# Gated attention and spatial-shift MLP mixer: a fixed engine order in the first token mixing block, fillers, and the MLP's first normalisation between the w2 products

## The chip, the cores and the metric

The kernel runs on one NeuronCore of a Trainium2 chip. The metric is the device time of one execution in microseconds (us). A core has five engines that matter here: TensorE (PE, matrix products; its weight loads are listed as PEld), VectorE (DVE), ScalarE (ACT, which evaluates functions such as gelu and exp from tables), GpSimd (POOL) and SyncE (SP, which here only issues DMA transfers). Each engine works through its own queue in order. Where it needs what another engine makes, it waits for a semaphore, and everything behind it in its queue waits too.

## The reference

```python
g  = sigmoid((x * gate_w).sum(-1))                # per token
# A: attention, 16 heads of 28 columns, one shared K and V
q = (x @ wq) -> 16 heads;  k = x @ wk;  v = x @ wv
a = softmax(q k^T * 28**-0.5) v -> concat -> @ wo
# B: spatial-shift mixer and MLP
h  = gelu(layernorm(x) @ w1)
hs = concat(h0 shifted +1, h1 shifted -1, h2 shifted +2, h3 shifted -2 tokens) @ w2
x1 = x + hs
b  = x1 + gelu(layernorm(x1) @ w3) @ w4
out = g * a + (1 - g) * b
```

x has S = 2048 tokens of D = 448 columns in fp32; w3 and w4 have an inner width of 1792. The layernorm has no scale or offset.

## The kernel before

Tokens are worked in 4 blocks of 512, each block in 4 tiles of 128 (16 tiles in all). To keep fp32 accuracy, most operands are split into a high part and a low remainder (names ending in h and l), and a product is summed from three: high by high, high by low, low by high. `proj` (L113 to L119) is one such sum of 11 matmuls over the 448 contracted columns. The fourth slice of 64 columns carries low parts in its other half, which saves one.

The work has three stages.

Stage 1, token mixing (about 0 to 130 us of the span). `stage_kv` (L247) makes k, v and the gate's sum in one product per block; `stage_q` (L278) makes the first two groups of q, whose parts are copied out by `q_evac` (L144: qh on ACT, ql on DVE, three DMAs to qs); `stage_v` (L270) transposes v into vext and the gate's sum into gz. The layernorm of block b is `ln1_begin` (L284), whose `layernorm_stats` (L121) runs four bn_stats and bn_aggr on DVE (L126, L127) and an add and a power on POOL (L128, L129) to get rs; and four `layernorm_tile` (L132): the normalised tile xn on DVE (L135), a copy of its last 64 columns on POOL (L137), four transposes on PE into tile tp (L140), and `split_a` (L108 to L111), which makes ah on ACT and al on DVE. `stage_w1` (L293) multiplies by w1 in four parts m, runs the normalisation tiles of the next block between them, and applies gelu twice on ACT (L304, L305); the low part hl comes from POOL (L306). `stage_w2` (L317) makes four tiles of the shifted product, 12 matmuls each (L322 to L324), and DVE adds each to x (L326). Lines 330 to 354 give the order. At its end the first MLP block is prepared: `ln_begin(0)`, `load_w34(i)` for the first four of seven pairs of w3 and w4 columns, and `ln_tile(0, t)` (the MLP's use of `layernorm_tile`). `load_w34` (L360) issues a DMA for w3 and one for w4 into a single buffer each, and splits them (w3h and w4h on ACT at L101 and L370, w3l on DVE at L104 and L105, w4l on POOL at L371). The order there is w2 of block 2, v of block 3, the further loads, `ln_tile(0, 0)`, then w2 of block 3 with the other three `ln_tile` between its tiles.

Stage 2, the MLP (about 130 to 424 us). For each block, 14 parts f: the product g with w3 (the lines of `proj`, L115 to L119), gelu twice (L409, L410), the low part gl (L411), and 12 matmuls with w4 into four accumulators (L419 to L421). At the end of a block DVE adds the accumulators to x (L449). Products of score maxima for the attention fill gaps.

Stage 3, attention (424 us to the end). First come the gate and the weights: gg = exp(-gz) on ACT (L456), gg + 1, its reciprocal, gi = 1 - gg on DVE (L457 to L459); wq is split (L576 to L587, high parts on DVE, low parts on POOL), the first block of x is loaded and split (`load_x(0)`, L483 to L491: ahq on DVE, alq on POOL), wo is split on POOL (L592, L593), and each tile of x is multiplied by gi on POOL (L595, L596: 16 instructions). The main loop (L646) runs 16 units of 16 key tiles: scores s on PE (L663), exp on ACT (L665), products with V on PE (L625). Further jobs are fed between the scores, a product at a time, by `pump`; the first is the q product of unit 2 (`q_job`, L493 to L509), from key tile 7 of the first unit on. Its second matmul (L503) reads alq.

PE's order is the order in which the code is written (a manual schedule of PE). The order of the other engines is chosen when the program is built, by a list scheduler that works by estimated times; an instruction written late may be put early if its inputs are there. So L456 and the first scalings of L596, which are written in stage 3, run during stage 2.

Of the kernel before, what the change touches and what calls it, by code (L numbers as in the profile page):

```python
# [15 lines left out]
P = 128  # L16
S = 2048
D = 448
# [17 lines left out]
def f32(ap):  # L36
    return ap.bitcast(F32)
# [3 lines left out]
def gated_mix_kernel(  # L41
# [32 lines left out]
    powt = keep.tile([P, 4], F32, name="powt")  # L74
    sel8 = keep.tile([P, P], F32R, name="sel8")
    mcs = [keep.tile([P, P], F32R, name=f"mc_{i}") for i in range(2)]
    nc.gpsimd.memset(epst, EPS)
    nc.gpsimd.memset(powt, -0.5)
    nc.gpsimd.memset(vext, 0.0)
    nc.gpsimd.memset(vext[:, :, 0:1], 1.0)  # L80
    nc.gpsimd.memset(f32(kS)[96:128, :], 1.0)
# [10 lines left out]
    def misc_tile(name):  # L92
        return psA.tile([P, 512], F32, tag="misc", bufs=1, name=name)

    wps = misc_tile("warm_ps")
    for _ in range(30):
        nc.tensor.matmul(wps[:, 0:256], warm[:, 0:P], warm, start=True, stop=True)

    def split_w(raw, wh, wl, eng=None):
        eng = eng or nc.vector  # L100
        nc.scalar.copy(wh[:, 0:3, :], raw[:, 0:3, :])  # L101
        nc.scalar.copy(wh[0:64, 3, :], raw[0:64, 3, :])
        nc.gpsimd.memset(f32(wh)[64:128, 3, :], 0.0)
        eng.tensor_tensor(wl[:, 0:3, :], raw[:, 0:3, :], f32(wh)[:, 0:3, :], ALU.subtract)  # L104
        eng.tensor_tensor(wl[0:64, 3, :], raw[0:64, 3, :], f32(wh)[0:64, 3, :], ALU.subtract)  # L105
        nc.scalar.copy(wl[64:128, 3, :], raw[64:128, 3, :])
# [6 lines left out]
    def proj(ps, wh, wl, ah, al):  # L113
        for c in range(3):
            nc.tensor.matmul(ps, wh[:, c, :], ah[:, c, :], start=(c == 0), stop=False)  # L115
            nc.tensor.matmul(ps, wh[:, c, :], al[:, c, :], start=False, stop=False)  # L116
            nc.tensor.matmul(ps, wl[:, c, :], ah[:, c, :], start=False, stop=False)  # L117
        nc.tensor.matmul(ps, wh[:, 3, :], ah[:, 3, :], start=False, stop=False)  # L118
        nc.tensor.matmul(ps, wl[:, 3, :], ah[:, 3, :], start=False, stop=True)  # L119
# [9 lines left out]
        nc.gpsimd.tensor_tensor(rs, rs, powt, ALU.pow)  # L129
        return mv, rs  # L130

    def layernorm_tile(pool, tp_of, b, t, mv, rs, ah, al):  # L132
        xt = x1[:, 4 * b + t, :]
        xn = pool.tile([P, 512], F32, tag="xn", bufs=3, name=f"xn_{pool.name}_{b}_{t}")
        nc.vector.tensor_scalar(xn[:, 0:D], xt, mv[:, t, 0:1], rs[:, t:t + 1],  # L135
                                op0=ALU.subtract, op1=ALU.mult)
        nc.gpsimd.tensor_copy(xn[:, D:512], xn[:, 384:D])  # L137
        tp = tp_of(f"tp_{pool.name}_{b}_{t}").rearrange("p (c n) -> p c n", c=4)
        for c in range(4):
            nc.tensor.transpose(tp[:, c, :], xn[:, c * P:(c + 1) * P], ident)  # L140
        cols = slice(t * P, (t + 1) * P)
        split_a(tp, ah[:, :, cols], al[:, :, cols])

    def q_evac(pool, u, ps, qs):  # L144
        qh = pool.tile([P, 512], F32R, tag="qh", bufs=2 if pool.name == "s1" else 1, name=f"qh_{u}")
        ql = pool.tile([P, 512], F32R, tag="ql", bufs=2 if pool.name == "s1" else 1, name=f"ql_{u}")
        nc.scalar.copy(qh, ps)
        nc.vector.tensor_sub(ql, ps, f32(qh))
        nc.sync.dma_start(f32(qs)[0:32], f32(qh))
        nc.sync.dma_start(f32(qs)[32:64], f32(ql))  # L150
        nc.sync.dma_start(f32(qs)[64:96], f32(qh))

    NU = NB * NG
    q_of = {}
# [48 lines left out]
    with tc.tile_pool(name="s1b", bufs=1) as s1b, \  # L203
# [40 lines left out]
        wql = s1.tile([P, 4, 256], F32R, name="wq01l")  # L244
        hh, hl, acts = {}, {}, {}

        def stage_kv(b):  # L247
            ah = s1.tile([P, 4, 512], F32R, tag="ah", bufs=2, name=f"ahk_{b}")
            al = s1.tile([P, 3, 512], F32R, tag="al", bufs=2, name=f"alk_{b}")
            if b == 0:  # L250
                for c in range(4):
                    nc.scalar.copy(ah[:, c, :], xraw[b][:, c, :])
                    if c < 3:
                        nc.vector.tensor_sub(al[:, c, :], xraw[b][:, c, :], f32(ah)[:, c, :])
                    else:
                        nc.vector.tensor_sub(ah[64:128, c, :], xraw[b][64:128, c, :], f32(ah)[64:128, c, :])
            else:
                split_a(xraw[b], ah, al)
            xact[b] = (ah, al)
            cols = slice(512 * b, 512 * b + 512)  # L260
            ps = max_tile(f"kv_{b}")[0:64, :]
            proj(ps, kvh, kvl, ah, al)
            nc.scalar.copy(kS[0:32, cols], ps[0:32, :])
            nc.scalar.copy(kS[32:64, cols], ps[0:32, :])
            nc.vector.tensor_sub(kS[64:96, cols], ps[0:32, :], f32(kS)[0:32, cols])
            vT = s1b.tile([32, 512], F32, tag="vT", bufs=1, name=f"vT_{b}")
            nc.scalar.copy(vT, ps[32:64, :])
            return vT

        def stage_v(b, vT):  # L270
            vp = misc_tile(f"vp_{b}")
            for t in range(4):
                nc.tensor.transpose(vp[:, 32 * t:32 * t + 32], vT[:, t * P:(t + 1) * P], ident[0:32, 0:32])
            vp = vp[:, 0:P].rearrange("p (t d) -> p t d", t=4)
            nc.vector.tensor_copy(vext[:, 4 * b:4 * b + 4, 1:1 + DH], vp[:, :, 0:DH])
            nc.vector.tensor_copy(gz[:, 4 * b:4 * b + 4], vp[:, :, DH])

        def stage_q(u):  # L278
            ps = mm_tile(f"q_{u}")
            proj(ps, wqh[:, :, u * P:(u + 1) * P], wql[:, :, u * P:(u + 1) * P], *xact[0])  # L280
            q_of[u] = keep.tile([P, 4, 512], F32R, name=f"qs_{u}", tag=f"qs{u}", bufs=1)
            q_evac(s1, u, ps, q_of[u])

        def ln1_begin(b):  # L284
            ah = s1.tile([P, 4, 512], F32R, tag="ah", bufs=2, name=f"ah1_{b}")
            al = s1.tile([P, 3, 512], F32R, tag="al", bufs=2, name=f"al1_{b}")
            acts[b] = (ah, al, *layernorm_stats(s1, b))

        def ln1_tile(b, t):
            ah, al, mv, rs = acts[b]  # L290
            layernorm_tile(s1, tp_tile, b, t, mv, rs, ah, al)

        def stage_w1(b):  # L293
            hh[b] = s1b.tile([P, 4, 516], F32R, tag="hh", bufs=2, name=f"hh_{b}")
            hl[b] = s1b.tile([P, 4, 516], F32R, tag="hl", bufs=2, name=f"hl_{b}")
            if b + 1 < NB:
                ln1_begin(b + 1)
            for m in range(4):
                ps = mm_tile(f"h_{b}_{m}")
                proj(ps[0:C, :], w1h[:, :, m * C:(m + 1) * C], w1l[:, :, m * C:(m + 1) * C], *acts[b][0:2])  # L300
                if b + 1 < NB:
                    ln1_tile(b + 1, m)
                hf = s1.tile([P, 512], F32, tag="hf", bufs=2, name=f"hf_{b}_{m}")
                nc.scalar.activation(hh[b][0:C, m, 2:514], ps[0:C, :], AF.Gelu_apprx_tanh)  # L304
                nc.scalar.activation(hf[0:C, :], ps[0:C, :], AF.Gelu_apprx_tanh)  # L305
                nc.gpsimd.tensor_tensor(hl[b][0:C, m, 2:514], hf[0:C, :], f32(hh[b])[0:C, m, 2:514],  # L306
                                        ALU.subtract)
            for tt in (hh, hl):
                if b == 0:
                    nc.gpsimd.memset(f32(tt[b])[0:C, :, 0:2], 0.0)  # L310
                else:
                    nc.gpsimd.tensor_copy(tt[b][0:C, :, 0:2], f32(tt[b - 1])[0:C, :, 512:514])
                    nc.gpsimd.tensor_copy(tt[b - 1][0:C, :, 514:516], f32(tt[b])[0:C, :, 2:4])
                if b == NB - 1:
                    nc.gpsimd.memset(f32(tt[b])[0:C, :, 514:516], 0.0)
# [11 lines left out]
                if between:  # L327
                    between(t)

        split_w(kvraw, kvh, kvl)  # L330
        vT = stage_kv(0)
        split_w(wqraw, wqh, wql, nc.gpsimd)
        stage_q(0)
        stage_v(0, vT)
        stage_q(1)
        ln1_begin(0)
        for t in range(4):
            ln1_tile(0, t)
        split_w(w1raw, w1h, w1l, nc.gpsimd)
        stage_w1(0)  # L340
        nc.scalar.copy(w2h[0:C], w2raw[0:C])
        nc.gpsimd.tensor_tensor(w2l[0:C], w2raw[0:C], f32(w2h)[0:C], ALU.subtract)
        stage_w1(1)
        stage_w2(0)
        load_x(2)
# [37 lines left out]

        ln_begin(0)
        load_w34(0, s2a)
        stage_w2(NB - 2)
        stage_v(3, vT)
        for i in range(1, 4):
            load_w34(i, s2a)
        ln_tile(0, 0, misc_tile)  # L390
        stage_w2(NB - 1, lambda t: ln_tile(0, t + 1, (misc_tile, max_tile)[t % 2]) if t < 3 else None)

    with tc.tile_pool(name="s2", bufs=1, reuse_waits="tile") as s2, \
            tc.tile_pool(name="ps2", bufs=1, space=PSUM, reuse_waits="tile") as ps2:
# [58 lines left out]

    with tc.tile_pool(name="s3", bufs=1, reuse_waits="tile") as s3, \
            tc.tile_pool(name="ps3", bufs=1, space=PSUM, reuse_waits="tile") as ps3:
        nc.scalar.activation(gg, gz, AF.Exp, scale=-1.0)  # L456
        nc.vector.tensor_scalar(gg, gg, 1.0, None, op0=ALU.add)  # L457
        nc.vector.reciprocal(gg, gg)
        nc.vector.tensor_scalar(gi, gg, -1.0, 1.0, op0=ALU.mult, op1=ALU.add)  # L459
# [350 lines left out]
```

## Time and profile before

| | |
|---|---|
| median of 3 runs | 1071.31 us (1070.52 to 1072.3) |
| the profiled execution | 1070.98 us; its span is 1069.1 us |
| mean granted TensorE clock | 0.987 |
| start of the w2 products of block 2 | 104.58 us |
| first score product of the attention | 423.94 us |
| gg (L456), gi (L459) | 119.3, 137.6 us |
| the 16 scalings of x (L596) | 211.6 to 430.2 us, shortest 1403 ns, median 1407 ns |
| table loads on ACT in the first 150 us | at 1.19, 26.14, 118.0 and 138.4 us, 1.28 us each |

The span runs from the first to the last instruction on the core; all positions below are microseconds from its start. A row of the timeline gives start, length, engine, line, operation, the output and input by name and shape, how many instructions it stands for, and in brackets how long the engine was idle before it and what released it. Matmuls are pipelined, so their pace is read from the distance between starts. The granted clock (PEclk) is the share of full speed at which PE was allowed to run, in tenths in the 40 slices of the span.

### The profile page before, as it was taken

What the parts mean: (1) busy time and instruction counts of PE and PEld (TensorE: products, weight loads), DVE (VectorE), ACT (ScalarE), POOL (GpSimd) and SP (SyncE); (2) the same over time, 40 slices, a digit from 0 to 9 for tenths busy, and PEclk for the clock granted to TensorE, in tenths of its full rate; (3) what the DMA queues carried; (4) which work ended last, traced back from release to release, by engine and by line L of the source; (5) the groups of instructions that cost most, each with busy time, mean ns of one, the idle gap of its engine ahead of it and who ended that gap; (6) DMA issues with size and microseconds to landing.
All of it is one profiled execution on the core that took longest, in us unless ns stands there. A gap on an engine that the chain in (4) does not pass through costs nothing.

```text
span 1069.1 us, 13948 instructions
## 1 busy us (share of the span) xinstructions
PE 1039.7 (97%) x5610; PEld 679.6 (64%) x5610; DVE 258.0 (24%) x521; ACT 673.2 (63%) x1318; POOL 159.8 (15%) x182
## 2 busy tenths in 40 slices
PE   6999889999999999999999999999999999999995
PEld 4787778888888888454554555554655555555542
DVE  6744952311411311401110110120110210111102
ACT  5444451222222223788888888889888889888873
POOL 5622430110200201603000002010002100000100
PEclk9999899999999999999999999999999999999998
DMA  9401330000000000423211202220202220211001
GB/s 312 131 1 37 111 111 1 1 1 1 1 1 1 1 1 29 164 32 70 33 17 16 31 20 40 39 31 3 39 10 41 39 31 2 40 24 26 10 2 38
DMA packets 30541, 41.15 MB, mean 38 GB/s; under 512 B 8004, under 2 KB 20100, under 8 KB 30340
## 3 DMA queue, kind: packets, MB, share of 16 engines
q1 hardware_dynamic: 30324, 40.04, 16.3%
q8 instruction: 46, 0.75, 0.3%
q14 instruction: 27, 0.22, 0.1%
q10 hardware_dynamic: 144, 0.13, 0.1%
HBM read 23.28 MB, written 3.67 MB: 25 GB/s over the span
## 4 chain that ended last, share of the span: by engine, by line
PE 91%; DVE 4%; DMA 1%; ACT 1%; POOL 1%; issue 1%; SPq 0%; POOLq 0%; ACTq 0%; DVEq 0%
PE s L663 27%; PE pv L625 22%; PE acc L420 4%; PE acc L419 4%; PE acc L421 4%; PE g L115 4%; PE g L116 4%; PE g L117 4%; PE q L503 3%; PE m L166 2%; PE wo L560 1%; PE wo L558 1%; PE wo L556 1%; PE g L119 1%; PE g L118 1%; PE h L116 1%
## 5 line engine op out<-in xcount | busy, mean ns | idle before, releaser
L665 ACT ACTIVATE p<-s 128x512 f32<-128x512 f32 x1024 | 517.6, 627 | 98.1 <-PE s L663 97.8
L663 PE MATMUL s<-qs,kS 98*128 98x512 f32 x1024 | 343.6, 420 | 1.4 <-ACT p L665 0.7
L663 PEld LDWEIGHTS s<-qs,kS 98*128 98x128 f32 x1024 | 181.6, 189 | 168.2 <-ACT p L665 127.1
L625 PE MATMUL pv<-p,vext 128*32 128x512 f32 x2048 | 247.6, 602 | 0.0
L409 ACT ACTIVATE gh<-g 128x512 fp32r<-128x512 f32 x56 | 33.6, 600 | 174.9 <-PE g L119 174.9
L625 PEld LDWEIGHTS pv<-p,vext 128*32 128x32 f32 x2048 | 53.7, 109 | 107.6 <-issue 100.3
L411 DVE TENSOR_TENSOR gl<-gf,gh 128x512 fp32r<-128x512 f32 x56 | 41.3, 738 | 192.1 <-ACT gf L410 192.0
L419 PE MATMUL acc<-w4h,gh 128*128 128x448 f32 x224 | 82.6, 369 | 0.0
L420 PE MATMUL acc<-w4l,gh 128*128 128x448 f32 x224 | 82.0, 366 | 0.0
L421 PE MATMUL acc<-w4h,gl 128*128 128x448 f32 x224 | 81.7, 365 | 0.0
L167 DVE TENSOR_REDUCE mr<-m 128x4 f32<-128x512 f32 x64 | 44.3, 692 | 146.0 <-PE m L166 145.3
L548 POOL CAST onh<-on 128x512 fp32r<-128x512 f32 x15 | 9.2, 614 | 414.8 <-DVE on L545 228.7
L115 PE MATMUL g<-ah,w3h 128*128 128x512 f32 x168 | 67.1, 399 | 3.1 <-ACT gf L410 2.8
L116 PE MATMUL g<-al,w3h 128*128 128x512 f32 x168 | 66.5, 396 | 0.1
L117 PE MATMUL g<-ah,w3l 128*128 128x512 f32 x168 | 66.3, 394 | 0.0
L521 DVE SCALAR_TENSOR_TENSOR good<-rt,good 128x16 f32<-128x16 f32 x15 | 2.6, 175 | 190.2 <-DMA rt<-o 190.2
L419 PEld LDWEIGHTS acc<-w4h,gh 128*128 128x128 f32 x224 | 42.0, 188 | 4.9
L420 PEld LDWEIGHTS acc<-w4l,gh 128*128 128x128 f32 x224 | 42.1, 188 | 4.8
L421 PEld LDWEIGHTS acc<-w4h,gl 128*128 128x128 f32 x224 | 42.0, 188 | 3.6
L166 PEld LDWEIGHTS m<-kS,qs 96*128 96x128 f32 x256 | 38.4, 191 | 6.3 <-DVE mr L167 1.2
L115 PEld LDWEIGHTS g<-ah,w3h 128*128 128x128 f32 x168 | 31.9, 190 | 9.7 <-ACT gf L410 3.3
L564 DVE SCALAR_TENSOR_TENSOR ot<-wo,gg,x 128x448 f32<-128x448 f32 x16 | 10.9, 682 | 108.0 <-PE wo L560 108.0
(204 smaller groups left out, 1144.4 us busy)
## 6 DMA issues: line engine op xcount, KB each, us to landing
qs<-qh SPq DMA_DIRECT2D x32, 256.0 KB
qs<-ql SPq DMA_DIRECT2D x16, 256.0 KB
xq<-in_xT_dram SPq DMA_DIRECT2D x4, 1024.0 KB
x<-in_x_dram SPq DMA_DIRECT2D x4, 896.0 KB
w3raw<-in_w_dram SPq DMA_DIRECT2D x7, 512.0 KB
out_dram<-ot SPq DMA_DIRECT2D x16, 224.0 KB
w4raw<-in_w_dram SPq DMA_DIRECT2D x7, 448.0 KB
xkv<-in_xT_dram SPq DMA_DIRECT2D x3, 1024.0 KB
```

Of the source, the lines that this page charges most:

```text
L115: nc.tensor.matmul(ps, wh[:, c, :], ah[:, c, :], start=(c == 0), stop=False)
L116: nc.tensor.matmul(ps, wh[:, c, :], al[:, c, :], start=False, stop=False)
L117: nc.tensor.matmul(ps, wl[:, c, :], ah[:, c, :], start=False, stop=False)
L166: nc.tensor.matmul(ps[:, j, :], q_of[u][0:96, j, t * P:(t + 1) * P], kS[0:96, 0:MK], start=True, stop=True)
L167: nc.vector.reduce_max(mx_of[u][:, :, t], ps, axis=AX.X)
L411: nc.vector.tensor_sub(gl, gf, f32(gh))
L419: nc.tensor.matmul(ps, gh[:, tok], w4h[i][:, k, :], start=(f == 0), stop=False)
L420: nc.tensor.matmul(ps, gh[:, tok], w4l[i][:, k, :], start=False, stop=False)
L421: nc.tensor.matmul(ps, gl[:, tok], w4h[i][:, k, :], start=False, stop=(f == NF - 1))
L625: nc.tensor.matmul(pv[32 * j:32 * j + 32, :], vext[:, kt, :], ps[j], start=(kt == 0), stop=(kt == NT - 1), tile_position=(0, 32 * j))
L663: nc.tensor.matmul(ps, kS[0:98, kt * P:(kt + 1) * P], q_of[u][0:98, j, :], start=True, stop=True)
L665: nc.scalar.activation(p, ps, AF.Exp, scale=SCALE)
```

## The change

- A small tile epst2 is written at the start by a gelu on ACT.
- The last 64 columns of xn are computed by a second DVE instruction instead of being copied by POOL. Stage 1 has four buffers for xn, one for ql.
- `q_evac` issues both qh transfers ahead of the ql one, and in stage 1 the ql part comes later.
- In the first block the order of PE, DVE, ACT and POOL is that of the program, rewritten: wq is split by halves, w1's low part in 8 pieces on POOL, the normalisation is begun before q, its xn tiles are made before and after q's parts, and each of its four groups of transposes is followed by 6 matmuls (128 by 256, bf16) whose result nobody reads.
- In the MLP's preparation `stage_v(3)` comes behind the first w2 tile of block 2, `ln_tile(0, 0)` to `(0, 2)` behind its other tiles, `ln_tile(0, 3)` behind it, then w2 of block 3 undivided, and the three further `load_w34` last.
- The exponential of the gate gets a bias of 0 that DVE computes from the last tile of x, after the MLP's last add to it.

With these the scheduler orders the engines anew. POOL's queue at the start of attention holds in before: two scalings of x, the memsets of rb, good and wqh, two scalings, four wql subtractions, alq, the fix of ahq, woh, wol. In the changed kernel it holds the memsets, 7 scalings, four wql subtractions, 6 scalings, alq, the fix of ahq, 2 scalings, woh, a scaling, wol. In the first block DVE makes all four al of block 0, then ql_1, and then the statistics of block 1; in before these are mixed. On ACT the first gelu of the MLP stands directly behind the w4h cast of the fourth pair, in before behind that of the fifth.

```diff
+    nc.scalar.activation(epst2, powt, AF.Gelu_apprx_tanh)
...
-    def layernorm_tile(pool, tp_of, b, t, mv, rs, ah, al):
+    def layernorm_xn(pool, b, t, mv, rs):
         xt = x1[:, 4 * b + t, :]
...
-        nc.gpsimd.tensor_copy(xn[:, D:512], xn[:, 384:D])
+        nc.vector.tensor_scalar(xn[:, D:512], xt[:, 384:D], mv[:, t, 0:1], rs[:, t:t + 1],
+                                op0=ALU.subtract, op1=ALU.mult)
+        return xn
...
-    def q_evac(pool, u, ps, qs):
+    def q_evac(pool, u, ps, qs, later=False):
...
         nc.scalar.copy(qh, ps)
-        nc.vector.tensor_sub(ql, ps, f32(qh))
         nc.sync.dma_start(f32(qs)[0:32], f32(qh))
-        nc.sync.dma_start(f32(qs)[32:64], f32(ql))
         nc.sync.dma_start(f32(qs)[64:96], f32(qh))
+
+        def low():
+            nc.vector.tensor_sub(ql, ps, f32(qh))
+            nc.sync.dma_start(f32(qs)[32:64], f32(ql))
...
-        split_w(kvraw, kvh, kvl)
-        vT = stage_kv(0)
-        split_w(wqraw, wqh, wql, nc.gpsimd)
-        stage_q(0)
-        stage_v(0, vT)
-        stage_q(1)
-        ln1_begin(0)
-        for t in range(4):
-            ln1_tile(0, t)
-        split_w(w1raw, w1h, w1l, nc.gpsimd)
-        stage_w1(0)
...
+        def split_wq():
+            for u in range(2):
+                w = slice(u * P, (u + 1) * P)
+                split_w(wqraw[:, :, w], wqh[:, :, w], wql[:, :, w], nc.gpsimd)
+
+        def split_w1():
+            nc.scalar.copy(w1h[:, 0:3, :], w1raw[:, 0:3, :])
+            nc.scalar.copy(w1h[0:64, 3, :], w1raw[0:64, 3, :])
+            nc.scalar.copy(w1l[64:128, 3, :], w1raw[64:128, 3, :])
+            nc.gpsimd.memset(f32(w1h)[64:128, 3, :], 0.0)
+            for m in range(4):
+                w = slice(m * C, (m + 1) * C)
+                nc.gpsimd.tensor_tensor(w1l[:, 0:3, w], w1raw[:, 0:3, w], f32(w1h)[:, 0:3, w], ALU.subtract)
+                nc.gpsimd.tensor_tensor(w1l[0:64, 3, w], w1raw[0:64, 3, w], f32(w1h)[0:64, 3, w], ALU.subtract)
+
+        with tc.manual_schedule(engines={mybir.EngineType.PE, mybir.EngineType.DVE,
+                                         mybir.EngineType.Activation, mybir.EngineType.Pool}):
+            split_w(kvraw, kvh, kvl)
+            vT = stage_kv(0, split_wq)
+            ln1_begin(0)
+            low0 = stage_q(0)
+            split_w1()
+            ah, al, mv, rs = acts[0]
+            xn = [layernorm_xn(s1, 0, t, mv, rs) for t in range(2)]
+            low0()
+            stage_v(0, vT)
+            low1 = stage_q(1)
+            xn += [layernorm_xn(s1, 0, t, mv, rs) for t in range(2, 4)]
+            idle = ps1.tile([P, 512], F32, tag="hs", bufs=2, name="idle")
+            for t in range(4):
+                layernorm_tile(s1, tp_tile, 0, t, mv, rs, ah, al, xn[t])
+                for _ in range(6):
+                    nc.tensor.matmul(idle[:, 0:256], warm[:, 0:P], warm, start=True, stop=True)
+            low1()
+            stage_w1(0)
...
         ln_begin(0)
         load_w34(0, s2a)
-        stage_w2(NB - 2)
-        stage_v(3, vT)
+        stage_w2(NB - 2, lambda t: ln_tile(0, t - 1, tp_tile) if t else stage_v(3, vT))
+        ln_tile(0, 3, tp_tile)
+        stage_w2(NB - 1)
         for i in range(1, 4):
             load_w34(i, s2a)
-        ln_tile(0, 0, misc_tile)
-        stage_w2(NB - 1, lambda t: ln_tile(0, t + 1, (misc_tile, max_tile)[t % 2]) if t < 3 else None)
...
-        nc.scalar.activation(gg, gz, AF.Exp, scale=-1.0)
+        nc.vector.tensor_scalar(epst2[:, 0:1], x1[:, NT - 1, 0:1], 0.0, 0.0, op0=ALU.max, op1=ALU.min)
+        nc.scalar.activation(gg, gz, AF.Exp, scale=-1.0, bias=epst2[:, 0:1])
```

More of the change, by code (lines that the diff above doesn't have):

```diff
@@ L76, in gated_mix_kernel @@
     mcs = [keep.tile([P, P], F32R, name=f"mc_{i}") for i in range(2)]
+    epst2 = keep.tile([P, 4], F32, name="epst2")
+    nc.gpsimd.memset(powt, -0.5)
     nc.gpsimd.memset(epst, EPS)
-    nc.gpsimd.memset(powt, -0.5)
     nc.gpsimd.memset(vext, 0.0)
@@ L130, in layernorm_stats, with layernorm_tile @@
         return mv, rs
[L132 removed]
+    def layernorm_xn(pool, b, t, mv, rs):
         xt = x1[:, 4 * b + t, :]
[L134 removed]
+        xn = pool.tile([P, 512], F32, tag="xn", bufs=4 if pool.name == "s1" else 3, name=f"xn_{pool.name}_{b}_{t}")
         nc.vector.tensor_scalar(xn[:, 0:D], xt, mv[:, t, 0:1], rs[:, t:t + 1],
                                 op0=ALU.subtract, op1=ALU.mult)
[L137 removed]
+        nc.vector.tensor_scalar(xn[:, D:512], xt[:, 384:D], mv[:, t, 0:1], rs[:, t:t + 1],
+                                op0=ALU.subtract, op1=ALU.mult)
+        return xn
+    def layernorm_tile(pool, tp_of, b, t, mv, rs, ah, al, xn=None):
+        xn = layernorm_xn(pool, b, t, mv, rs) if xn is None else xn
         tp = tp_of(f"tp_{pool.name}_{b}_{t}").rearrange("p (c n) -> p c n", c=4)
@@ L142, in layernorm_tile @@
         split_a(tp, ah[:, :, cols], al[:, :, cols])
-    def q_evac(pool, u, ps, qs):
+    def q_evac(pool, u, ps, qs, later=False):
         qh = pool.tile([P, 512], F32R, tag="qh", bufs=2 if pool.name == "s1" else 1, name=f"qh_{u}")
-        ql = pool.tile([P, 512], F32R, tag="ql", bufs=2 if pool.name == "s1" else 1, name=f"ql_{u}")
+        ql = pool.tile([P, 512], F32R, tag="ql", bufs=1, name=f"ql_{u}")
         nc.scalar.copy(qh, ps)
-        nc.vector.tensor_sub(ql, ps, f32(qh))
         nc.sync.dma_start(f32(qs)[0:32], f32(qh))
-        nc.sync.dma_start(f32(qs)[32:64], f32(ql))
         nc.sync.dma_start(f32(qs)[64:96], f32(qh))
+        def low():
+            nc.vector.tensor_sub(ql, ps, f32(qh))
+            nc.sync.dma_start(f32(qs)[32:64], f32(ql))
+        if later:
+            return low
+        low()
     NU = NB * NG
@@ L245, in gated_mix_kernel, with stage_kv @@
         hh, hl, acts = {}, {}, {}
-        def stage_kv(b):
+        def stage_kv(b, before=None):
             ah = s1.tile([P, 4, 512], F32R, tag="ah", bufs=2, name=f"ahk_{b}")
@@ L262, in stage_kv @@
             proj(ps, kvh, kvl, ah, al)
+            if before:
+                before()
             nc.scalar.copy(kS[0:32, cols], ps[0:32, :])
@@ L279, in stage_q @@
             ps = mm_tile(f"q_{u}")
-            proj(ps, wqh[:, :, u * P:(u + 1) * P], wql[:, :, u * P:(u + 1) * P], *xact[0])
+            w = slice(u * P, (u + 1) * P)
+            proj(ps, wqh[:, :, w], wql[:, :, w], *xact[0])
             q_of[u] = keep.tile([P, 4, 512], F32R, name=f"qs_{u}", tag=f"qs{u}", bufs=1)
-            q_evac(s1, u, ps, q_of[u])
+            return q_evac(s1, u, ps, q_of[u], True)
         def ln1_begin(b):
@@ L328, in stage_w2 @@
                     between(t)
-        split_w(kvraw, kvh, kvl)
-        vT = stage_kv(0)
-        split_w(wqraw, wqh, wql, nc.gpsimd)
-        stage_q(0)
-        stage_v(0, vT)
-        stage_q(1)
-        ln1_begin(0)
-        for t in range(4):
-            ln1_tile(0, t)
-        split_w(w1raw, w1h, w1l, nc.gpsimd)
-        stage_w1(0)
-        nc.scalar.copy(w2h[0:C], w2raw[0:C])
-        nc.gpsimd.tensor_tensor(w2l[0:C], w2raw[0:C], f32(w2h)[0:C], ALU.subtract)
+        def split_wq():
+            for u in range(2):
+                w = slice(u * P, (u + 1) * P)
+                split_w(wqraw[:, :, w], wqh[:, :, w], wql[:, :, w], nc.gpsimd)
[28 more added lines that the diff above has]
+            stage_w1(0)
+            nc.scalar.copy(w2h[0:C], w2raw[0:C])
+            nc.gpsimd.tensor_tensor(w2l[0:C], w2raw[0:C], f32(w2h)[0:C], ALU.subtract)
         stage_w1(1)
```

## The prediction

> **What bounds the kernel now.** I first read the busy times by engine and the 40 slices.
>
> ```profile
> PE 1039.7 (97%) x5610; PEld 679.6 (64%) x5610; DVE 258.0 (24%) x521; ACT 673.2 (63%) x1318; POOL 159.8 (15%) x182
> PE   6999889999999999999999999999999999999995
> PEclk9999899999999999999999999999999999999998
> ```
>
> TensorE (PE) is busy 97% of the span, and the chain of work that ended last lies 91% on it. PE runs its queue strictly in order, so a stall is time lost unless a later stall shrinks. The windows by stage show where PE is not busy (columns: length; busy PE, PEld, DVE, ACT, POOL; granted clock; DMA share; GB/s).
>
> ```profile
> 0.00:42.00 42.00, 31.57 (x144) 21.79 (x144) 30.47 (x72) 22.61 (x37) 25.39 (x44) 0.92 0.93 282
> 105.00:146.00 41.00, 35.11 (x154) 29.85 (x153) 32.18 (x66) 22.06 (x37) 19.64 (x26) 0.88 0.43 127
> 424.00:1069.10 645.10, 632.87 (x3698) 337.30 (x3696) 100.31 (x223) 532.26 (x1076) 70.17 (x55) 0.99 0.18 34
> ```
>
> Idle PE time is 10.4 us in the first stretch, 5.9 in the second (the end of token mixing with the MLP's first normalisation), and 12.2 in the attention stretch, much of it its tail. Between 146 and 424 PE is idle under 0.5 us. So the change can win only in the first two stretches, and anything late for PE in the others costs its full length.
>
> **What the change does, part by part.** PE's instruction list is the same but for 24 fillers and moved transposes; the other engines' orders are read from the two programs.
>
> **1. The gate's Exp is pinned behind the MLP (the main term).** Before, gg (L456) runs during the MLP, so 12 of the 16 scalings of x by gi (L596, POOL) run there too, after each block's last x add (76.1 us of POOL idle ahead of L596). Only four are left at attention's start. The timeline of POOL there (start, length, operation, idle before):
>
> ```profile
> 423.03 2.79 POOL L596 TENSOR_SCALAR x<-x,gi 128x448 f32<-128x448 f32 x2 [62.91 <-DVE x L449]
> ...
> 427.48 2.79 POOL L596 TENSOR_SCALAR x<-x,gi 128x448 f32<-128x448 f32 x2
> 430.24 1.86 POOL L582 TENSOR_TENSOR wql<-wqraw,wqh 128x768 fp32r<-128x768 f32 x1
> 432.06 0.77 POOL L583 TENSOR_TENSOR wql<-wqraw,wqh 64x256 fp32r<-64x256 f32 x1
> 433.46 1.84 POOL L582 TENSOR_TENSOR wql<-wqraw,wqh 128x768 fp32r<-128x768 f32 x1 [0.63 <-DVE wqh L580]
> ...
> 437.35 3.49 POOL L489 TENSOR_TENSOR alq<-xq,ahq 128x1536 fp32r<-128x1536 f32 x1 [1.32 <-DVE ahq L488]
> ```
>
> And PE's row that needs it:
>
> ```profile
> 440.95 0.44 PE L503 MATMUL q<-alq,wqh 128*128 128x512 f32 x1
> ```
>
> alq ends at 440.84 and PE uses it at 440.95: this hand-over has no slack, 17.0 us after attention begins at 423.94.
>
> After, Exp takes as its bias a value that VectorE (DVE) writes from the last x tile of the MLP, so nothing of gi exists before the last x add. All 16 scalings then fall into attention, and POOL's queue holds, in order: two rb memsets, good, the wqh memset, 7 scalings, the four wql subtractions, 6 scalings, alq, the ahq fix, 2 scalings, woh, a scaling, wol. POOL, too, runs in order, so 13 scalings stand ahead of alq. Step by step: the last x add ends at 424.76 (422.32 + 2.44); the bias, Exp and three small gate operations (0.15 to 0.6 each, by like rows) make gi ready near 426.0, 2.0 after the start. 13 scalings take 13 x 1.395 (2.79 / 2) to 13 x 1.445 (5.78 / 4, inside the MLP), 18.1 to 18.8. The wql work takes 5.2 (1.86 + 0.77 + 1.84 + 0.78), alq 3.49. alq ends at 2.0 + 18.4 + 5.2 + 3.5 = 29.1, or up to 31.6 where wql and alq wait for DVE's casts as before (0.63 + 1.32, and starts a little late). PE asks for it at 17.3 (17.0, and 0.3 for Exp between the first p tiles on ScalarE, ACT). **The wait is 11.9 to 14.3; I take 13.0.**
>
> Behind a wait of this kind PE runs slowly at first. In before, after the 2.71 us wait below, the w2 products of 118.5 to 123.1 came 0.373 apart against 0.205 later: 12 x 0.17 = 2.0 us; after the 2.83 us wait the same costs 1.4. I add 2.0 (0 to 3.4, half pace for a stretch as long as that from 24.43 to 31.2 below). The Trainium skill ("TensorE: Matmul & The Clock Gate", Part 1) says that a fully idle window of about 3.4 us drops TensorE to half clock until a busy window has passed. The trace agrees on the halving, but waits of 2.7 and 2.8 us were enough here; by that rule the 13 us wait costs up to 1.7, by the rows 1.4 to 2.0.
>
> Can it be won back? PE's waits from 424 to the end sum to 2.7 us, mostly in the tail, and nothing there shrinks. (ACT's exponentials, 98 us of idle ahead of them, are no help: they wait for PE.) **Term 1: 13.0 + 2.0 + 0.3 = +15.3, bounds 12.5 to 18.**
>
> **2. The first block (0 to 42).** PE's losses are these waits (total, times, longest) and a slow clock from 24.43 to 31.2, in which the h products came 0.43 apart against 0.23: about 2.0.
>
> ```profile
> PE vp L273 <- ACT vT L267: 1.6, 1, 1.6
> PE h L116 <- DVE al L110: 1.6, 1, 1.6
> PE h L115 <- ACT ah L109: 1.4, 2, 0.7
> PE q L117 <- POOL wq01l L104: 1.2, 1, 1.2
> ```
>
> Won: wq split by halves gives q_0's third product about 1.3 earlier (0.95 for half of 1.81); vT no longer sits behind the w1h cast (1.31), so vp comes near 12.8 rather than 14.8; POOL's 64-column copies (0.24 to 0.45 each) leave the path; the gelu table (1.28 at 26.14) is loaded at the start. Fillers fill PE between the four transposes; they shift no consumer. Lost: DVE now does all four al subtractions before any statistics of block 1. By replaying the order with the rows' durations, the first h product group ends between 26.2 and 28.9, but tp of block 1 needs behind al: ql (0.67), four bn_stats and aggr (0.6 + 0.17 each, 3.0), the two rs operations (0.20 + 1.03), an xn (0.51 + 0.2): 6.4 with hand-overs. It starts at 30.3 to 32.9, where before it was 31.20. So PE's waits move to there, one of about 3.7, with a slow clock behind it again. The spread is the port between DVE and POOL:
>
> ```profile
> 27.10 3.62 DVE L135 TENSOR_SCALAR xn_s<-x,mv_s,rs_s 128x448 f32<-128x448 f32 x1
> 26.47 3.99 POOL L342 TENSOR_TENSOR w2l<-w2raw,w2h 112x1792 fp32r<-112x1792 f32 x1
> ```
>
> An xn that takes 0.51 elsewhere took 3.62, ending as POOL's w2l did: it stood still for POOL. After, w1l runs on POOL in 8 pieces just where the four xn (two instructions each now) run on DVE, so each may wait for a piece. The Trainium skill ("SBUF — State Buffer", the section on its two sides) says that these engines share a pair of ports, and whichever starts first holds it for its whole instruction. By that rule giving the copy to DVE doubles the instructions that can be held; the rows agree, and which of them is held is a race that no row settles. Bounds: no holding and no slow clock -1.2; all held +5.5, with up to 0.55 for each of three xn behind hl. **I take +2.5**, near the middle: the slow clock after a wait of this size was seen three times.
>
> **3. The MLP's first normalisation between the w2 products (105 to 146).** Lost before:
>
> ```profile
> PE g L115 <- ACT gf L410: 2.8, 1, 2.8
> PE tp_s2a L140 <- DVE gz L276: 2.7, 1, 2.7
> PE g L115 <- ACT ah L109: 0.3, 1, 0.3
> ```
>
> With the slow clocks (2.0 and 1.4) and 0.3 at the first g, 9.5 us. The 2.83 goes: its gelu stood behind a table load and the w4h cast of the fifth pair, and now stands ahead of both. The 2.71 doesn't go: tp_0 is asked for 5.6 after the w2 products begin, while its xn is held by w4l as before
>
> ```profile
> 110.80 2.12 POOL L371 TENSOR_TENSOR w4l<-w4raw,w4h 128x896 fp32r<-128x896 f32 x1
> 110.86 2.30 DVE L135 TENSOR_SCALAR xn_s2a<-x,mv_s2a,rs_s2a 128x448 f32<-128x448 f32 x1
> ```
>
> and its second piece follows w3l (0.94 + 0.41) and an x add (0.60), at 9.85 by the same replay: 3.9 idle and 2.0 of slow clock. With 0.3 at vp and 0.4 at a later g, 6.6. **Term 3: 6.6 - 9.5 = -3**, bounds -6.6 (xn starts ahead of w4l, and the clock holds) to 0.
>
> **4. The rest: 0.** The MLP from 146 to 424 keeps its PE list and loses 12 scalings that were off the path. The new order of the q_0 and q_1 transfers on SP is hidden by 140 us of other work (issued by 23.1, qs is first read at 165.1); were it late, PE's score-maximum products would wait for it. The gelu load at the start takes the place of the copy's load at 1.19, ahead of the first transfer.
>
> **Sum.** 15.3 + 2.5 - 3.0 = +14.8. The profiled execution took 1070.98 (span 1069.1 and 1.9 around it), 0.33 under the median of the runs: 1070.98 + 14.8 = 1085.8, **1086**.
>
> **The rivals.**
> A, the first stretches replay better than I think (no holding, no slow clocks): -1.2 - 6.6 + 12.5 = +4.7, 1076. For it: whichever engine is first takes the port. Against: before was held at both places.
> B, they replay worse: +5.5 + 0 + 18 = +23.5, 1094.
> C, **faster**: alq is not late. From gi to PE's request there are 17.3 - 2.0 - 5.2 - 3.5 = 6.6 for 13 scalings, so it decides from 0.51 us each. All 16 rows are about 1.4 (shortest 1.403), 2.8 times that. Then only +0.3, +2.5 and -3 are left, at best 0.3 - 1.2 - 6.6: 1063 to 1071.
> D, the change doesn't do what it says: the pinned Exp frees the MLP from two table loads (118.0 and 138.4), and the scalings end up behind alq; the order read says otherwise, and this too gives C's time.
>
> **How the numbers follow.** Forecast 0.74, A 0.09, B 0.09, C and D together 0.08. Two tenths of a per cent, about 2 us, is what a measurement of this kernel can tell from no change. All of the forecast, A and B is slower; of the 0.08, most is faster: faster 0.06, same 0.02, slower 0.92. The range takes in the forecast and most of A and B: 1075 to 1094.
>
> **What would show it.** Right: one PE wait of about 13 us near 441 at q<-alq, released by POOL's L489; POOL's rows of scalings in runs of 7 and 6, and wql between; a dip of the granted clock right behind; in the first 42 us a wait of some 3.7 at a transpose of block 1; the 2.8 at g<-gf gone, and a wait of about 4 at the MLP's first transpose. Wrong: alq landing before PE's request, scalings under 1 us, or a POOL order with alq ahead of the scalings. If the stall is there and the total is off by over 5 us, term 2 or 3 was mis-sized, and PE's idle time by stage tells which.

## The result, and the profile after

The changed kernel takes 1100.3 us (median of 4, 1098.0 to 1101.01) against 1071.8 us: a ratio of 1.0264, 95% interval 1.0246 to 1.0283. It is slower, as forecast, but by 28.5 us and not by 14.8, and outside the range. The page's first lines show it as more idle PE and a lower clock.

```profile
span 1097.8 us, 13999 instructions
...
PE 1050.8 (96%) x5634; PEld 686.2 (63%) x5634; DVE 271.4 (25%) x554; ACT 670.2 (61%) x1319; POOL 154.7 (14%) x159
...
PE   7699889999999999699999999999999999999996
...
PEclk8899899999999999789999999999999999999998
```

Two dips stand out: slices 1 to 6, and slices 17 and 18 (440 to 490 us, attention's start). To see how much each holds, take three marks that both traces have: the first w2 product of block 2, the first score product, and the end.

| stretch | before | after | difference | forecast |
|---|---|---|---|---|
| start to the w2 products of block 2 | 104.58 | 118.02 | **+13.4** | +2.5 |
| from there to attention | 319.36 | 320.26 | **+0.9** | -3.0 |
| attention to the end | 645.16 | 659.52 | **+14.4** | +15.3 |

The last row came as forecast; the first is where 11 of the 14 missing us went. PE's waits in the three places (total, times, longest), from three answers of the waits view of the changed kernel: 0 to 60, 60 to 150, and the rest.

```profile
PE tp_s L147 <- DVE xn_s L137: 10.0, 3, 6.4
PE tp_s L147 <- DVE ah L113: 1.3, 1, 1.3
```

```profile
PE tp_s2a L147 <- DVE xn_s2a L137: 2.0, 1, 2.0
PE tp_s2a L147 <- DVE xn_s2a L139: 1.2, 1, 1.2
```

```profile
PE q L543 <- POOL alq L529: 11.9, 1, 11.9
PE g L117 <- ACT gf L449: 2.6, 1, 2.6
PE acc L460 <- DVE gl L450: 1.6, 1, 1.6
```

In the first block PE waits under 1 us each for vT, wq's low part and al, which before cost it 1 to 2 us each; it waits 10.0 us for xn. L137 is the first of the two DVE instructions that make xn, L139 the second.

**Attention.** POOL's timeline there:

```profile
440.52 11.03 POOL L636 TENSOR_SCALAR x<-x,gi 128x448 f32<-128x448 f32 x7 [7.92 <-DVE gi L499]
451.53 1.83 POOL L622 TENSOR_TENSOR wql<-wqraw,wqh 128x768 fp32r<-128x768 f32 x1
...
456.51 8.31 POOL L636 TENSOR_SCALAR x<-x,gi 128x448 f32<-128x448 f32 x6
464.79 3.42 POOL L529 TENSOR_TENSOR alq<-xq,ahq 128x1536 fp32r<-128x1536 f32 x1
```

Thirteen scalings take 19.3 us, alq ends at 468.21, and PE starts the product that reads it at 468.26, 11.9 us late:

```profile
468.26 0.79 PE L543 MATMUL q<-alq,wqh 128*128 128x512 f32 x1 [11.86 <-POOL alq L529]
```

**The first block.** DVE's timeline, three rows:

```profile
18.77 3.13 DVE L137 TENSOR_SCALAR xn_s<-x,mv_s,rs_s 128x448 f32<-128x448 f32 x1
...
33.28 0.69 DVE L159 TENSOR_TENSOR ql<-q,qh 128x512 fp32r<-128x512 f32 x1 [2.75 <-DMA qs<-ql]
...
38.71 0.51 DVE L137 TENSOR_SCALAR xn_s<-x,mv_s,rs_s 128x448 f32<-128x448 f32 x1 [0.91 <-POOL rs_s L131]
```

Two things are to be seen. The second xn of block 0 took 3.13 us where others take 0.5: POOL's w1l pieces ran from 17.89 on. It stood through at least four of them in a row (18.76 to 21.27), so cutting w1l into pieces did not let it in between. And ql of unit 1 waited 2.75 us for the transfer of ql of unit 0, since there is one buffer now; behind it in DVE's queue stand all statistics of block 1, and PE's first transpose of that block came at 39.37 (before: 31.20). Followed along PE's queue, the loss grows like this:

| PE starts | before | after | later by |
|---|---|---|---|
| first h product of block 0 | 24.46 | 29.92 | 5.5 |
| first transposes of block 1 | 31.20 | 39.37 | 8.2 |
| second transposes of block 1 | 34.19 | 44.57 | 10.4 |
| first transposes of block 2 | 44.77 | 57.98 | 13.2 |
| w2 products of block 2 | 104.58 | 118.02 | 13.4 |

The first two steps are the held xn, the fillers and the wait of ql. The next two are mostly slow clock behind PE's waits: the h products came 0.43 us apart from 40.7 to 43.7 and from 54.7 to 57.3, against 0.23 elsewhere.

### The profile page after: what moved, and what is told of

Read it like the earlier page. It is cut to its first block, busy times and chain, and to the rows that moved or that the text cites. A ratio compares the mean times of both kernels' runs of the same rounds, so it can differ in the third digit from the quotient of the medians.

```text
span 1097.8 us, 13999 instructions
## 1 busy us (share of the span) xinstructions
PE 1050.8 (96%) x5634; PEld 686.2 (63%) x5634; DVE 271.4 (25%) x554; ACT 670.2 (61%) x1319; POOL 154.7 (14%) x159
## 4 chain that ended last, share of the span: by engine, by line
PE 87%; DVE 3%; POOL 3%; DMA 3%; ACT 2%; issue 1%; SPq 0%; POOLq 0%; DVEq 0%; ACTq 0%
PE s L703 25%; PE pv L665 21%; PE acc L458 4%; PE acc L459 4%; PE acc L460 4%; PE g L117 3%; PE g L119 3%; PE g L118 3%; PE q L543 3%; PE m L179 2%; POOL x L636 1%; PE wo L600 1%; PE wo L598 1%; PE wo L596 1%; PE g L121 1%
## 5 line engine op out<-in xcount | busy, mean ns | idle before, releaser
L705 ACT ACTIVATE p<-s 128x512 f32<-128x512 f32 x1024 | 517.6, 627 | 113.1 <-PE s L703 112.8
L588 POOL CAST onh<-on 128x512 fp32r<-128x512 f32 x15 | 9.2, 616 | 414.3 <-DVE on L585 318.1
```

Source lines behind the costliest of these rows:

```text
L705: nc.scalar.activation(p, ps, AF.Exp, scale=SCALE)
```

## The experiments

All times are medians with the ratio to the kernel before on the same chip; the three columns are the stretches of the table above, from each run's trace.

| run | to w2 | to attention | to the end | median, ratio [95%] |
|---|---|---|---|---|
| e6 | 116.6 | 321.5 | 645.0 | 1084.8, 1.0111 [1.0094, 1.0128] |
| e1 | 105.2 | 318.1 | 658.9 | 1085.2, 1.0123 [1.0106, 1.0140] |
| e3 | 115.5 | 321.3 | 660.9 | 1098.6, 1.0239 [1.0222, 1.0256] |
| e4 | 114.4 | 320.1 | 659.2 | 1095.3, 1.0215 [1.0198, 1.0232] |
| f1 | 104.8 | 313.4 | 658.3 | 1081.4, 1.0083 [1.0064, 1.0102] |
| f4 | 104.9 | 312.6 | 645.0 | 1064.4, 0.9924 [0.9904, 0.9943] |
| e5 | 105.2 | 315.1 | 646.7 | 1068.1, 0.9955 [0.9939, 0.9971] |
| b1 | 104.9 | 318.3 | 645.4 | 1070.0, 0.9975 [0.9964, 0.9987] |
| g1 | 116.2 | 313.9 | 643.7 | 1077.1, 1.0044 [1.0031, 1.0058] |
| g2 | 109.4 | 315.3 | 643.7 | 1068.4, 0.9955 [0.9936, 0.9973] |
| g3 | 106.1 | 315.5 | 643.9 | 1067.7, 0.9945 [0.9927, 0.9964] |
| g4 | 117.5 | 320.3 | 659.7 | 1096.8, 1.0220 [1.0199, 1.0240] |
| h1 | 112.8 | 320.8 | 659.3 | 1095.8, 1.0227 [1.0199, 1.0255] |
| h2 | 114.4 | 322.0 | 645.6 | 1082.6, 1.0089 [1.0055, 1.0122] |

### Attention: e6 and e1

e6 wraps the weights' splits, load_x(0) and the scalings in a fixed order of POOL, so that the scalings come last:

```diff
+        with tc.manual_schedule(engines={mybir.EngineType.PE, mybir.EngineType.Pool}):
             nc.gpsimd.memset(f32(wqh)[64:128, 3, :], 0.0)
             split_wq(2, 4)
             load_x(0)
...
             for n in range(NT):
                 nc.gpsimd.tensor_scalar(x1[:, n, :], x1[:, n, :], gi[:, n:n + 1], None, op0=ALU.mult)
```

> The changed kernel with POOL's order at the start of attention fixed: memsets, two wql subtractions, alq, the fix of ahq, the other wql, woh, wol, and all 16 scalings of x behind them. Theory 1 (the attention loses its time because 13 scalings stand ahead of alq on POOL): the 11.9 us wait of q for alq goes, with the slow pace behind it, about 14 us in all: 1086 us. Rival (the late Exp itself, or later readers of the scaled x, set the loss, and the wait only shows it): the wait moves to the first gated output and at most 3 us come back, 1097 us or more.

Measured 1084.8, 15.5 less. The attention stretch is 645.0, that of before; the longest wait of PE left in it, from the waits view:

```profile
PE s L704 <- ACT p L706: 1.0, 3, 0.5
```

e1 puts the two lines of the pinned Exp into the kernel before, and nothing else.

> The kernel before with the gate's Exp alone pinned behind the MLP's last add, nothing else of the change. POOL's queue then has 7 scalings, wql, 6 scalings, alq. Theory 1: the attention begins up to 2.7 us earlier, as two table loads of 1.28 us leave the MLP's start, and then loses the wait for alq and its slow pace, 14 us: 1083 to 1086 us. Rival (the wait needs the other parts of the change): 1069 to 1073 us.

Measured 1085.2: attention starts 0.7 us earlier and then takes 658.9. So the pin is enough for the whole loss there, and the place of the scalings on POOL is its cause.

### The first block: e3, f1, h2, h1

e3 gives the first block its old program order (two ql buffers, three xn, no fillers), and keeps the second DVE instruction.

> The changed kernel with the first block in the program order of before (statistics and tiles behind q, w1 and wq split whole, no fillers, two ql buffers, three xn), the scheduler ordering DVE, ACT and POOL; the second DVE instruction for the last 64 columns of xn stays. Theory 2 (the fixed order of the first block costs the 13.4 us by which the w2 products of block 2 begin later): 13 us come back, 1087 us, and those products begin near 104.6. Rival (the 64 columns on DVE cost it, through the port that DVE and POOL share): less than half comes back, 1094 us or more.

Measured 1098.6. Theory 2, that the fixed order is the cause, falls: only 2.6 of the 13.4 us came back. The trace says why, POOL's timeline first, then DVE's:

```profile
15.90 3.07 POOL L106 TENSOR_TENSOR w1l<-w1raw,w1h 128x1344 fp32r<-128x1344 f32 x1
...
31.42 4.01 POOL L358 TENSOR_TENSOR w2l<-w2raw,w2h 112x1792 fp32r<-112x1792 f32 x1
```

```profile
15.97 3.26 DVE L137 TENSOR_SCALAR xn_s<-x,mv_s,rs_s 128x448 f32<-128x448 f32 x1 [1.44 <-POOL rs_s L131]
...
31.50 4.18 DVE L137 TENSOR_SCALAR xn_s<-x,mv_s,rs_s 128x448 f32<-128x448 f32 x1 [1.42 <-POOL rs_s L131]
```

Both engines start right behind POOL's power. POOL is first by 0.07 and 0.08 us, and xn ends only behind the long subtraction, by 0.26 and 0.25 us. f1 is e3 with the 64 columns copied by POOL again:

```diff
-        nc.vector.tensor_scalar(xn[:, D:512], xt[:, 384:D], mv[:, t, 0:1], rs[:, t:t + 1],
-                                op0=ALU.subtract, op1=ALU.mult)
+        nc.gpsimd.tensor_copy(xn[:, D:512], xn[:, 384:D])
```

> The run with the old first block, and the last 64 columns of xn copied by POOL again. With the second DVE instruction POOL had nothing to wait for between the power and w1l: w1l began at 15.90, xn at 15.97, and xn took 3.26 us; in the kernel before the copy, which needs xn, stood ahead of w1l and held POOL back until xn was done. Theory 3 (the copy on POOL is an interlock that keeps POOL's long subtractions off the xn instructions; both the fixed order and the removal of the copy lose it): the w2 products of block 2 begin near 104.6 again, against 115.45, and the time falls by 10 to 12 us to 1087 to 1089 us. Rival (the remaining loss of that run lies in the order of al, the statistics and the tiles, with no part of the copy): under 3 us come back, 1096 us or more.

Measured 1081.4, 17 less than e3: the first stretch is 104.8 again, and the second fell by 7.9 more, which I had not counted. The rows of the same place show the old state; they are from f4, which differs from f1 in attention alone (POOL, then DVE):

```profile
16.41 0.45 POOL L139 COPY xn_s<-xn_s 128x64 f32<-128x64 f32 x1 [0.61 <-DVE xn_s L137]
16.83 3.29 POOL L106 TENSOR_TENSOR w1l<-w1raw,w1h 128x1344 fp32r<-128x1344 f32 x1
```

```profile
15.84 1.36 DVE L137 TENSOR_SCALAR xn_s<-x,mv_s,rs_s 128x448 f32<-128x448 f32 x3 [1.43 <-POOL rs_s L131]
```

The copy needs xn, stands ahead of w1l in POOL's queue, and so keeps w1l back until xn is made; three xn pass in 1.36 us. It worked as an interlock: it held one engine back until the other was done. It guards only the xn ahead of it. The second xn of block 1 was held by w2l in the kernel before too (3.62 us, the row in the prediction), but there PE needed it only at 34.19. h2 tests the move alone, in the kernel before.

> The kernel before with the last 64 columns of xn computed by a second DVE instruction as the only edit. Theory 3: w1l, w2l and w4l stand directly behind the power on POOL and hold xn in block 0, block 1 and ahead of the MLP; as with the old block in the changed kernel, the w2 products of block 2 begin about 10 us later: 1080 to 1088 us. Rival (the loss needs other parts of the change): 1072 to 1076 us.

Measured 1082.6: the w2 products begin at 114.4, 9.9 later. POOL's and DVE's rows:

```profile
15.97 3.07 POOL L104 TENSOR_TENSOR w1l<-w1raw,w1h 128x1344 fp32r<-128x1344 f32 x1
```

```profile
16.04 3.25 DVE L135 TENSOR_SCALAR xn_s<-x,mv_s,rs_s 128x448 f32<-128x448 f32 x1 [1.43 <-POOL rs_s L129]
```

The move is the only edit, but the list scheduler answers it with another order on DVE: the fourth of block 1's statistics runs at 28.42, where before it ran at 19.62. e3 and h1 have this order too, f1 and f4 that of before. So these runs price the copy as a whole, 9.9 us here, and do not separate the hold from the new order; g1 below has an order fixed by hand. h1 tests the interlock without the copy: in e3, POOL reads one element per partition of each finished xn.

```diff
+        nc.gpsimd.tensor_copy(epst2[:, 1:2], xn[:, 511:512])
```

> The run with the old first block (1098.6; the 64 columns on DVE), with one more POOL instruction per tile that reads one element per partition of what the second DVE instruction wrote, into a scratch nobody reads. In POOL's order it stands ahead of w1l for tile 0 of block 0, but behind w2l for block 1 and behind w4l for the MLP's first block. Theory 3 (what the copy did was to hold POOL's long instruction back until xn is done, and the number of DVE instructions matters little): w1l begins behind xn_0, xn_0 takes 0.5 us instead of 3.3 and the first h product comes 2 to 3.5 us earlier, while the xn of block 1 and of the MLP stay held by w2l and w4l (4 and 2 us): 1094 to 1097 us. Rival (the second DVE instruction itself costs the time): the first h product stays near 28.7 and the time at 1098 us or more.

Measured 1095.8, and DVE's and POOL's timelines:

```profile
15.74 0.51 DVE L137 TENSOR_SCALAR xn_s<-x,mv_s,rs_s 128x448 f32<-128x448 f32 x1 [1.44 <-POOL rs_s L131]
...
16.81 3.20 DVE L139 TENSOR_SCALAR xn_s<-x,mv_s,rs_s 128x64 f32<-128x64 f32 x1
...
30.70 4.18 DVE L137 TENSOR_SCALAR xn_s<-x,mv_s,rs_s 128x448 f32<-128x448 f32 x1 [1.42 <-POOL rs_s L131]
```

```profile
16.90 3.06 POOL L106 TENSOR_TENSOR w1l<-w1raw,w1h 128x1344 fp32r<-128x1344 f32 x1
```

xn of tile 0 is free, as theory 3 has it, and the xn of block 1, which has no reader ahead of w2l, is held as before. But the hold in block 0 did not vanish: it went to the second, 64-column instruction of tile 1. So by these rows both halves count: the missing interlock, and the added instructions, which stretch the xn work over the start of w1l.

### Inside the fixed order: e4, g1, g2, g3, g4

e4 gives ql of unit 1 a second buffer (that of hf, not in use yet).

> The changed kernel with a second buffer for ql of unit 1 in the first block. DVE sat idle 2.7 us ahead of ql_1, released by the transfer of ql_0. Theory 2a (that wait, with all of block 1's statistics queued behind it, is part of the first block's loss): 2.7 to 4 us come back, 1096 to 1097.5 us. Rival (the statistics of block 1 are held by something else just as long): under 1 us comes back, 1099.5 us or more.

Measured 1095.3, 5.0 less than the change (3.6 of it in the first stretch): more than the 2.75 us of DVE's wait. PE's first transposes of block 1 come 2.9 us earlier, the second ones 3.5. g1 to g3 keep the fixed order, with the copy on POOL, the w1l pieces behind the four copies, and POOL's order of e6; g2 adds the buffer, g3 drops the fillers as well.

> The changed kernel with the fixed order of the first block kept, but the last 64 columns of xn copied by POOL and the 8 pieces of w1l behind these copies in POOL's order; POOL's order at the start of attention fixed as before (alone that gave 1084.8). One buffer for ql stays. Theory 3: the four xn of block 0 take 0.5 us each again, h begins 3 to 5 us earlier; the wait of ql_1 for the transfer of ql_0 (2.7 us) stays or grows. The w2 products of block 2 begin near 109 to 112 and the MLP's first transpose waits under 1 us instead of 3.4: 1068 to 1074 us. Rival (it is the order of al and the statistics that costs the fixed block its time): 1080 us or more.

Measured 1077.1, slower than expected. The first h product starts at 23.19, against 29.92 in the change. Here the order is fixed by hand, and the copy with w1l behind it is all that differs in the first block. So these 6.7 us are not the scheduler's: they are the hold, the four added instructions (0.3 us each) and PE's slow pace behind them. With xn free, all four al end by 24.1, and the wait for the transfer comes out in full, on DVE and on PE:

```profile
33.44 0.69 DVE L158 TENSOR_TENSOR ql<-q,qh 128x512 fp32r<-128x512 f32 x1 [9.39 <-DMA qs<-ql]
```

```profile
39.53 1.08 PE L146 MATMUL tp_s<-ident,xn_s 128*128 128x128 f32 x4 [13.20 <-DVE xn_s L137]
```

In the changed kernel it was 2.75 us because the held xn had made DVE late already: two causes in a row, of which the second hid behind the first. So the first block's gain is lost again at this wait, and the w2 products begin at 116.2.

> The same with a second buffer for ql of unit 1. Theories 2a and 3 together: DVE no longer waits for the transfer, block 1's statistics follow al_3 at once, and the w2 products of block 2 begin at 103 to 106: 1063 to 1067 us, level with the old block in the program order (1064.4). Rival (the fixed order has a cost of its own beyond the two, the statistics standing behind all four al): 1068 us or more.

Measured 1068.4; the w2 products begin at 109.4, still 4.5 behind the old order of f4, and the time is just over the bound I had set. The rival holds here: PE still waits 3.8 us for the first xn of block 1, whose statistics stand behind all four al and ql.

> The same without the 24 fillers. Theory 5a (the fillers hold PE's clock up in the block's gaps): 1 to 2 us slower than with them. Theory 5b (they delay transposes that are ready, 0.8 to 1.5 us a group of six): 1 to 2 us faster. Within 0.5 us: neither matters once the waits are short.

Measured 1067.7 against 1068.4, intervals that overlap, though the first stretch is 3.3 shorter in the profiled execution (that of g2 is the slowest of its five). What is left to f4 there is 1.2 us.

> The changed kernel without the 24 fillers and nothing else. In its trace each group of six took 1.1 to 1.3 us at the slow pace and the last two stood ahead of tp_3 and the first h product. Theory 5b: 1 to 2.5 us faster, 1098 to 1099.3 us. Theory 5a: slower, over 1101 us.

Measured 1096.8 against 1100.3, more than expected; the first stretch of the profiled execution, the slowest of the four at 1099.4, is only 0.5 shorter. The fillers win nothing in either kernel; how much they cost stays open within some 3 us.

### The second stretch and the version that wins: e5, b1, f4

> The kernel before with the MLP's first normalisation between the w2 products of block 2, and the loads behind, as the only edit; Exp stays free. Theory 4 (the wait at g is not removed but moved, since the gelu pairs now stand behind casts of weights that are loaded later): within 2 us of before, 1070.5 to 1074 us. Rival (the term of the prediction, a gain of 3 us): 1068 to 1070 us.

Measured 1068.1: theory 4 falls. Alone, moving the normalisation between the w2 products is worth 4.2 us in its stretch, as PE's first transpose waits 0.4 us there and not 2.7.

> The kernel before with the gate's Exp pinned and all 16 scalings behind alq on POOL. Theory 1: the stall at alq is gone, and the two table loads of 1.28 us stay out of the MLP's start, where g waited 2.83 us behind one of them: 1070 to 1071.5 us, a little faster than before. Rival (the scalings, now within the first unit of attention, hold DVE or POOL for what PE needs there): 1073 us or more.

Measured 1070.0: with the scalings out of the way the pinned Exp is a small gain. PE's wait at g did not go, though: it is 2.7 us here, for al.

> The same with POOL's order at the start of attention fixed so that all 16 scalings stand behind alq. What is left of the change: the gelu at the start, the qh transfers ahead of ql's, the normalisation between the w2 products, the pinned Exp. Theories 1 and 3 together: 14 us less than the run without the POOL order, 1072 to 1075 us, and the rest of the change is worth about nothing. Rival (the two losses share a cause and don't add up): 1078 us or more.

f4 is f1 with POOL's order of e6. Measured 1064.4, ratio 0.9924: 0.8% faster than the kernel before, and better than expected. Its waits in the second stretch:

```profile
PE g L117 <- ACT gf L424: 0.8, 2, 0.5
...
PE tp_s2a L146 <- POOL xn_s2a L139: 0.4, 1, 0.4
```

## Why the prediction was wrong

**Term 1, the pinned Exp: right.** +14.4 measured, +15.3 forecast; alq ended 29.9 after attention's start (forecast 29.1), PE's wait was 11.9 (13.0 taken, 11.9 the low end). The mechanism is shown by e6 and e1. PE asked later than I had it, at 18.1 and not at 17.3.

**Term 2, the first block: this step failed.** It said "+2.5", bounds -1.2 and +5.5; it measured +13.4. Three things were wrong in it.

First, the hold. The prediction named the port, but treated which engine holds it as an even race with a middle, and listed the copies only as something that "leave the path". What they kept back stood nowhere in its sum. Without them nothing on POOL waits for xn: in e3 and h2 POOL's next long subtraction starts right behind the power, with xn 0.07 us behind it. In the changed kernel three of the eight xn instructions of block 0 were held by w1l, 3.8 us in all beyond their usual 0.5 and 0.3. The replay had the first h group end between 26.2 and 28.9 and the first transposes of block 1 at 30.3 to 32.9; they came at 33.0 and 39.4. Against g1 the first h product is 6.7 us late; h2 prices the removal of the copies alone at 9.9 us in this stretch. The sentence from the Trainium skill ("SBUF — State Buffer", "SBUF: two separate sides": whichever engine starts first keeps the shared pair for its whole instruction; on DVE's side the page limits this to instructions in a 2-port mode or with two SBUF inputs) agrees with the held rows of w1l and w2l in e3 and h2. In h1 the held row begins 0.09 us ahead of w1l, but the xn before it runs until 16.89, so the starts of the rows do not settle who came first there. The sentence was cited, and its consequence was not followed through.

Second, the single ql buffer, which stands in the diff, was not priced at all; part 4 put the transfers at 0 because qs is read late, and did not ask who waits for the buffer. ql of unit 1 waits for a transfer issued at 23.33 whose end DVE sees at 33.28. A second buffer gave 3.6 us in this stretch in e4, and 6.8 from g1 to g2, where xn is free.

Third, "fillers shift no consumer" does not hold: at the slow clock each group took 1.1 to 1.3 us, and the last two stood directly ahead of the fourth tile's transposes and of h. What this cost stays open (g3, g4).

**Term 3: the sign failed with term 2.** -3.0 forecast, +0.9 measured. As forecast, the first transpose waited 3.2 us behind an xn held by w4l (2.26 us); what was not forecast is that the wait at g stayed in size and moved (2.6 at g and 1.6 at the accumulators, against 2.8 before). That the held xn decides it is shown by f1 against e3: 313.4 against 321.3 with only the copy changed. The working "held by w4l as before" was right for this kernel and missed that the edit is good without it: 4.2 us in e5, 6.7 in f4, where Exp is pinned as well.

**Slips in the sums.** Three figures of the prediction do not come out of its own rows, and none changes the result. The lower bound of term 1 should be 12.2 (11.9 + 0 + 0.3) and not 12.5. The parts of term 3's loss before sum to 9.2 and not 9.5. vp in the kernel before starts at 15.39 and not at 14.8, which is when ACT begins to copy vT.

**The rivals.** B, at 1094, was the nearest, for the wrong sum. C's point of decision (0.51 us a scaling) was never near: a scaling took 1.49. D did not happen.

## What to carry to other kernels

Before an instruction is moved off an engine, ask what it made that engine wait for: a small copy that needs another engine's result can be the one thing that keeps a long instruction behind it from starting too early. Count every buffer that a change takes away as a wait for its last reader, a DMA too, and price what stands behind that wait in the queue; and when two such waits lie in a row, mending the first alone brings out the second. A list scheduler fills an idle engine with whatever is ready, so work that loses its early slot has to be given a place.

## What the runs showed of the hardware

A held DVE instruction lasts as long as what holds it: 3.26 beside a 3.07 us POOL subtraction, 4.18 beside 4.01, against 0.5 alone; and in the changed kernel one stood through several short ones in a row. Not every DVE instruction is held: in the kernel before, statistics (0.59) and ql (0.68) kept their usual length while w1l ran from 16.75 to 20.06.

The fillers did not remove the slow clock, they moved it. The windows view of g2 (with them) and g3 (without), the granted clock third from the end:

```profile
23.00:30.00 7.00, 3.51 (x16) 1.99 (x13) 5.71 (x15) 0.41 (x1) 3.65 (x6) 0.91 1.07 294
30.00:36.00 6.00, 5.55 (x17) 4.25 (x18) 5.12 (x14) 1.57 (x3) 2.88 (x5) 0.53 1.05 231
```

```profile
23.00:30.00 7.00, 5.20 (x11) 3.13 (x11) 5.66 (x15) 0.34 (x1) 3.52 (x6) 0.58 1.08 256
30.00:36.00 6.00, 5.21 (x26) 4.00 (x27) 5.72 (x16) 2.92 (x6) 2.88 (x5) 1.00 1.06 200
```

With fillers the first h products run fast, PE reaches its next wait earlier, waits 3.8 us instead of 1.8, and runs slowly behind it. Where the next input comes at a fixed time (the first xn of block 1 starts at 29.79 and 29.71), the fast stretch was bought for nothing.
